# Expert weights of a soft mixture of experts read as 12 KB per partition, with the slots and inner columns reordered

## The chip, the cores and the metric

The kernel runs on one core of one Trainium2 chip. The metric is the device time of one execution in microseconds (us). Three runs of the kernel before gave 594.96, 595.63 and 597.86 us; their median is 595.63 us.

## What is computed

The program computes a causal attention, a soft mixture of experts ("soft MoE") on its output, and a gated two-layer network on that. The change touches the second part only. Cut to what matters:

```python
# N = 1792 tokens, D = 768, E = 8 experts, 4 slots each, F = 1024
logits = x @ phi                          # x: attention output, N x D
d = softmax over tokens of logits
slot_input = (d.T @ x).reshape(E, 4, D)
for e in range(E):
    h = np.maximum(slot_input[e] @ w1[e], 0.0)     # w1[e]: 768 x 1024
    slot_out[e] = h @ w2[e]                        # w2[e]: 1024 x 768
c = softmax over slots of logits
return c @ slot_out                       # goes into the gated network
```

All arrays are float32, except that the three weight matrices of the last network arrive as float64 and are converted on the chip (`from_f64`).

## The kernel before

**Three stages.** Up to about 256 us the attention runs, with an order of steps written out in a table of times (`AT`, `TAIL`, `LOADS`). Its tail ends in `slotT` (lines 630 to 634): six matmuls with `acc` (the sum over tokens, 128 x 768) as stationary operand make the 32 slots' inputs, transposed, 128 rows by six chunks of 32. From there to about 346 us the expert stage runs (lines 754 to 813). After it the gated network runs in six parts (`gate`, `outp`, `prep`).

**Weight pieces.** All weights go through one list, `worder` (lines 156 to 167). Each entry is one DMA of 1536 KB into a tile `w` of 128 x 3072 float32. An expert has four pieces: two of w1 (three chunks of 128 rows each) and two of w2 (four chunks of 128 rows each). I number the pieces in that order: 0 to 3 are expert 0 (w1, w1, w2, w2), and so on to 23, the last of expert 5. Then come 24 to 26, the first w_out, w_val and w_gate of the gated network (unit 0), then 27 to 34 for experts 6 and 7, then unit 1. All are issued by SP (line 181), in this order and pinned to it.

**How a piece lies in memory before.** `w1[e].rearrange("(k p) f -> p k f", p=128)` puts row 128k + p on partition p, so one partition receives three separate rows of 4 KB from each w1 piece, and four rows of 3 KB from each w2 piece.

**Buffers.** The first ten pieces are loaded during the attention, one per step of two head pairs (lines 623 and 624). For the rest `ring` hands out the buffers (lines 170 and 638 to 649): 10 to 14 go into memory that the attention gives back, 15 to 17 into the buffers of 0 to 2, 18 to 24 into those of 3 to 9, 25 to 28 into those of 10 to 13, 29 to 31 into those of 15 to 17, 32 to 34 into those of 18 to 20. So piece 15 waits until the matmuls on piece 0 are done, and piece 17 until those on piece 2 are.

**The matmuls on them.** For each expert (line 757), each of six row chunks kc and each of four column groups g, line 762 multiplies 32 slots with 256 columns of w1 into `psh`: the group g owns partitions 32g to 32g+31. In the trace each of these fp32 matmuls shows as two instructions, and the four groups run side by side; I call four of them that start together a round. Line 765 applies the ReLU and a mask that keeps the expert's own slots; line 768 transposes the result, line 770 copies it out (`hT`), and line 775 multiplies eight chunks of it with the rows of w2, in three column groups, into `so`, which sums over all experts. At the end `so` becomes `soT` (line 813), which the gated network multiplies with its weights (line 688). There the weights are the upper halves of converted float64 values, so the matmul reads every second float32, that is, with a step of 8 bytes.

**The order around it.** The instruction order of each engine comes from a scheduler with a cost model, except for the pinned instructions.

Of the kernel before, what the change touches and what calls it, by code (L numbers as in the profile page):

```python
# [20 lines left out]
def kernel(  # L21
# [13 lines left out]
    nc = tc.nc  # L35
# [6 lines left out]
    KC = DM // 128  # L42
# [71 lines left out]
    g = nc.gpsimd  # L114
# [34 lines left out]
    def w_unit(u):  # L149
        out_ = [(("o", u), w_out.bitcast(I32).rearrange("(k p) f -> p k f", p=128)[:, 2 * u:2 * u + 2, :], 2)]  # L150
        for nm, w in (("v", w_val), ("g", w_gate)):
            src = w.bitcast(I32)[:, 2 * UC * u:2 * UC * (u + 1)]
            out_.append(((nm, u), src.rearrange("(k p) f -> p k f", p=128), KC))
        return out_

    worder = []
    for e in range(E):
        if e == E0:
            for u in PARTS[0]:
                worder += w_unit(u)  # L160
        for r in range(2):
            worder.append((("1", e, r), w1[e].rearrange("(k p) f -> p k f", p=128)[:, 3 * r:3 * r + 3, :], 3))
        for r in range(2):
            worder.append((("2", e, r), w2[e].rearrange("(k p) f -> p k f", p=128)[:, 4 * r:4 * r + 4, :], 4))
    n_ab = len(worder)
    for u in range(len(PARTS[0]), FF // UC):
        worder += w_unit(u)
# [18 lines left out]
    def from_f64(key):  # L186

        t = wt[key].bitcast(I32).rearrange("p a (b w) -> p a b w", w=2)  # L190
        lo, hi = t[:, :, :, 0], t[:, :, :, 1]
        top = wt[key].bitcast(U16).rearrange("p a (b w) -> p a b w", w=4)[:, :, :, 1]

        nc.scalar.activation(out=lo, in_=top, func=AF.Copy, scale=2.0 ** -13, bias=2.0 ** -15 - 0.5)  # L194
        yield
        mult("A", hi.bitcast(F32), hi.bitcast(F32), 2.0 ** -112)
        yield
        nc.vector.scalar_tensor_tensor(lo, hi, -2 ** 31, lo, ALU.bitwise_and, ALU.bitwise_or)  # L198
        yield
        nc.vector.scalar_tensor_tensor(hi, hi, 3, lo, ALU.logical_shift_left, ALU.bitwise_or)  # L200
        yield
        return hi.bitcast(F32)


    with ExitStack() as actx:
# [17 lines left out]
        acc = ac_p.tile([128, DM], F32, name="acc")  # L223
# [28 lines left out]
        fin = {}  # L252
# [377 lines left out]
        slotT = const.tile([128, KC, NS], F32, name="slotT")  # L630
        p4 = psT.tile([128, KC, NS], F32, tag="t", name="psm4")
        for kc in range(KC):
            nc.tensor.matmul(p4[:, kc], lhsT=acc[:, 128 * kc:128 * kc + 128], rhs=fin["fw"], start=True, stop=True)
        nc.vector.tensor_copy(slotT, p4)


# [25 lines left out]
    def prep_o(u, wo):  # L662

        d = unit[u]
        mw = sm1("mw")
        wh = wo_p[u].tile([128, 2, DM], F16, tag=f"wh{(u - 1) % 4}", name="wh")
        wl = wo_p[u].tile([128, 2, DM], F16, tag=f"wl{(u - 1) % 4}", name="wl")
        if MWE[u] == "A":
            nc.scalar.activation(out=wl, in_=wo, func=AF.Abs, accum_out=mw)
        else:  # L670
            nc.vector.tensor_reduce(mw, wo, axis=AX.XY, op=ALU.max, apply_absolute_value=True)
        yield
        am = spread_sum(sm2, ps1, "a", mw)
        d["pw"], sw = pow2(sm2, am, 1, f"w{u}")
        mult(WHE[u], wh, wo, sw)
        yield
        nc.vector.scalar_tensor_tensor(wl, wo, sw, wh, ALU.mult, ALU.subtract)
        d["w"] = (wh, wl)
        yield
# [77 lines left out]
    for e in range(E):  # L757
        ps = ps1.tile([128, 256], F32, tag="a", name="psh")
        for kc in range(KC):
            w = wt["1", e, kc // 3]  # L760
            for g in range(4):
                nc.tensor.matmul(ps[32 * g:32 * g + 32, :], lhsT=slotT[:, kc, :],  # L762
                                 rhs=w[:, kc % 3, 256 * g:256 * g + 256], start=kc == 0, stop=kc == KC - 1)
        hm = hm_p.tile([128, 256], F32, tag="hm", name="hm")
        nc.vector.tensor_scalar(hm, ps, 0.0, emask[:, e:e + 1], ALU.max, ALU.mult)
        pt = ps1.tile([128, 2, 128], F32, tag="b", name="psht")
        for i in range(2):
            nc.tensor.transpose(pt[:, i], hm[:, 128 * i:128 * i + 128], ident)  # L768
        hT = hm_p.tile([128, 2, 128], F32, tag="hT", name="hT")
        nc.scalar.copy(hT, pt)  # L770
        for f in range(8):
            g, i = divmod(f, 2)
            w = wt["2", e, f // 4]
            for c in range(3):
                nc.tensor.matmul(so[32 * c:32 * c + 32, :], lhsT=hT[:, i, 32 * g:32 * g + 32],  # L775
                                 rhs=w[:, f % 4, 256 * c:256 * c + 256],
                                 start=e == 0 and f == 0, stop=e == E - 1 and f == 7)
        if e < B:
            b = e
            cs = cs_p.tile([128, 4, 2, 2, NS], F32, tag="cs", name="cs")  # L780
            chi = hm_p.tile([128, 4, NS], F32R, tag="chi", name="chi")
            c = call[:, b]
            nc.vector.tensor_copy(chi, c)
            ch = chi.bitcast(F32).rearrange("p j (o s) -> p j o s", o=1).to_broadcast([128, 4, 2, NS])
            c4 = c.rearrange("p j (o s) -> p j o s", o=1).to_broadcast([128, 4, 2, NS])
            nc.vector.tensor_copy(cs[:, :, :, 0, :], ch)
            nc.vector.tensor_tensor(cs[:, :, :, 1, :], c4, ch, ALU.subtract)
            ps = ps1.tile([128, S], F32, tag="b", name="psc")
            for j, (s0, n) in enumerate(CH):
                nc.tensor.transpose(ps[:, s0:s0 + n], cs[:n, j].rearrange("p a b s -> p (a b s)"), ident[:n, :n])  # L790
            nc.scalar.copy(cT[:, b * S:(b + 1) * S], ps)
        if e == E0 - 1:
            once.close()
            wo0 = ctx.enter_context(rp("wo0", 1))
            wo_p.update({u: wo0 for u in PARTS[0]})
            w0 = {}
            for u in PARTS[0]:
                for nm in "ovg":
                    f = from_f64((nm, u))
                    while True:  # L800
                        try:
                            next(f)
                        except StopIteration as x:
                            w0[nm, u] = x.value
                            break
                for _ in prep_o(u, w0["o", u]):
                    pass
# [151 lines left out]
```

## Time and profile before

| | |
|---|---|
| median of three runs | 595.63 us |
| shortest, longest | 594.96, 597.86 us |
| span of the profiled execution, first to last instruction | 595.0 us |
| TensorE busy | 514.5 us (86%) |
| VectorE, ScalarE, GpSimd busy | 390.0, 322.6, 238.7 us |
| mean granted TensorE clock | 0.945 of full speed |
| HBM read, written | 95.26 MB, 5.51 MB |
| DMA queue q1 | 95504 packets, 100.77 MB, 51.3% of 16 engines' span |

The profiled execution has no time of its own beside its span; the span is within 0.1 us of the shortest of the three runs and 0.6 us below their median. In the profile PE is TensorE's matmuls, PEld its weight loads, DVE VectorE, ACT ScalarE, POOL GpSimd and SP the engine that issues the DMAs; an engine name with a q at its end (SPq) is that engine's own instruction queue. "L762" is line 762 of the kernel. A DMA share of 1.00 or a little above means that all 16 DMA engines are busy.

### The profile page before, as it was taken

To read this page: it belongs to the slowest core of one execution; us is meant where nothing else is said; L and a number is where in the kernel's file an instruction comes from. 1 tells how busy PE (TensorE), PEld (TensorE's weight loads), DVE (VectorE), ACT (ScalarE), POOL (GpSimd) and SP (SyncE) were. 2 spreads that over 40 slices of the span, in tenths; PEclk is the share of its full clock that TensorE was granted. 3 is DMA by queue.
4 is the path that set the end of the run, shared out by engine and by line. 5 is a ranking of instruction groups with operands and counts; after the bars stand their busy time and mean duration, and the time that the engine had idled before them with its cause. 6 is when DMAs were issued, how large, how long until landed. Compare 5 with 4: busy or idle time off the path is not lost.

```text
span 595.0 us, 12947 instructions
## 1 busy us (share of the span) xinstructions
PE 514.5 (86%) x4971; PEld 317.2 (53%) x4971; DVE 390.0 (66%) x943; ACT 322.6 (54%) x738; POOL 238.7 (40%) x333
## 2 busy tenths in 40 slices
PE   2899989998999899799935689679999989899997
PEld 1576756665667566465512235344554445455654
DVE  3688877886878687331027038986895958675664
ACT  2577767776777577301043049996865843334300
POOL 6654663656365410000000014206696760355720
PEclk9899999999999899979995789998999979799999
DMA  7746557464774313779999993713505303000044
GB/s 161 200 106 170 167 160 199 129 144 133 199 196 115 91 33 107 287 251 391 405 397 405 405 400 137 281 38 119 200 1 209 110 2 107 0 1 1 2 185 186
DMA packets 95566, 101.59 MB, mean 171 GB/s; under 512 B 68625, under 2 KB 68625, under 8 KB 95505
## 3 DMA queue, kind: packets, MB, share of 16 engines
q1 hardware_dynamic: 95504, 100.77, 51.3%
q8 instruction: 39, 0.64, 0.5%
q14 instruction: 23, 0.18, 0.1%
HBM read 95.26 MB, written 5.51 MB: 169 GB/s over the span
## 4 chain that ended last, share of the span: by engine, by line
PE 63%; ACT 15%; DMA 7%; DVE 5%; issue 3%; POOL 2%; SPq 1%; ACTq 0%; DVEq 0%; POOLq 0%
PE pso L870 22%; PE psP L244 9%; PE psS L244 8%; DMA w<-in_moe_w_dram 6%; ACT P L244 4%; PE psX L244 4%; PE psT L244 4%; PE psh L762 3%; PE so L775 3%; ACT hi L244 3%; ACT oacc L144 2%; ACT w L194 2%; PE psg L688 2%; PE psg L843 1%; ACT w L144 1%
## 5 line engine op out<-in xcount | busy, mean ns | idle before, releaser
L852 POOL TENSOR_TENSOR hlo<-hs,hhi 128x448 f16<-128x448 f32 x48 | 59.2, 1241 | 174.9 <-DVE hhi L851 132.5
L870 PE MATMUL pso<-wh,hhi 128*128 128x384 f16 (+1 forms) x384 | 111.5, 338 | 8.1 <-ACT oacc L144 7.6
L870 PE MATMUL pso<-wl,hhi 128*128 128x384 f16 (+1 forms) x384 | 110.3, 334 | 0.0
L870 PE MATMUL pso<-wh,hlo 128*128 128x384 f16 (+1 forms) x384 | 107.8, 331 | 2.6 <-POOL hlo L852 2.6
L244 ACT ACTIVATE P<-psS,nm 128x256 f32<-128x256 f32 (+3 forms) x168 | 82.0, 504 | 31.4 <-PE psP L244 16.6
L870 PEld LDWEIGHTS <-hhi 128*128 128x128 f16 (+1 forms) x768 | 63.5, 103 | 63.8 <-issue 32.3
L244 DVE CUSTOM_DVE_ANT_0 psS<-psS,cmaskq,sc 128x256 f32<-128x256 f32 (+1 forms) x144 | 66.5, 489 | 32.7 <-PE psS L244 30.2
L882 DVE SCALAR_TENSOR_TENSOR oacc<-pso,osc,oacc 128x384 f32<-128x384 f32 x98 | 58.7, 613 | 35.1 <-PE pso L870 34.6
L244 PE MATMUL psP<-ident,P 128*128 128x128 f32 x384 | 59.6, 288 | 17.7 <-ACT P L244 11.6
L880 POOL TENSOR_TENSOR oacc<-oacc,ev 128x384 f32<-128x384 f32 x42 | 55.0, 1321 | 23.1 <-ACT ev L144 23.0
L244 PEld LDWEIGHTS psP<-ident,P 128*128 128x128 f32 x384 | 41.3, 142 | 35.9 <-ACT P L244 21.5
L244 POOL TENSOR_TENSOR sq<-sq 128x512 bf16<-128x512 bf16 (+1 forms) x88 | 56.3, 640 | 6.5
L244 PE MATMUL psV<-PT,v 128*64 128x64 f32 (+3 forms) x672 | 48.0, 293 | 0.3 <-ACT PT L244 0.3
L870 PEld LDWEIGHTS <-hlo 128*128 128x128 f16 (+1 forms) x384 | 34.1, 102 | 26.1 <-issue 3.5
L198 DVE SCALAR_TENSOR_TENSOR w<-w 128x1536 int32<-128x1536 int32 x18 | 33.7, 1874 | 14.5 <-ACT w L144 14.1
L244 PEld LDWEIGHTS psV<-PT,v 128*64 128x64 f32 x672 | 32.0, 137 | 20.9 <-issue 14.0
L144 ACT ACTIVATE ev<-pso,osc 128x384 f32<-128x384 f32 x42 | 23.6, 581 | 27.4 <-PE pso L870 23.7
L194 ACT ACTIVATE w<-w 128x1536 int32<-128x1536 uint16 x18 | 30.2, 1680 | 14.9 <-DMA w<-in_moe_w_out_dram 7.9
L244 POOL TENSOR_SCALAR r<-sum 128x7 f32<-128x7 f32 x24 | 5.9, 244 | 79.1 <-ACT P L244 71.9
L762 PE MATMUL psh<-w,slotT 128*32 128x256 f32 x384 | 29.9, 441 | 7.8 <-DMA w<-in_moe_w_dram 7.3
L244 ACT ACTIVATE hi<-psT,qks 128x448 f16<-128x448 f32 x48 | 27.8, 630 | 15.2 <-PE psT L244 15.2
L770 ACT COPY hT<-psht 128x256 f32<-128x256 f32 x8 | 3.0, 372 | 61.0 <-PE psht L768 61.0
(233 smaller groups left out, 1000.7 us busy)
## 6 DMA issues: line engine op xcount, KB each, us to landing
w<-in_moe_w_dram SPq DMA_DIRECT2D x32, 1536.0 KB, 9.3
w<-in_moe_w_out_dram SPq DMA_DIRECT2D x6, 1536.0 KB, 12.2
w<-in_moe_w_val_dram SPq DMA_DIRECT2D x6, 1536.0 KB, 13.4
w<-in_moe_w_gate_dram SPq DMA_DIRECT2D x6, 1536.0 KB, 6.7
out_dram<-oacc SPq DMA_DIRECT2D x14, 384.0 KB, 2.3
q<-in_q_dram SPq DMA_DIRECT2D x36, 128.0 KB, 3.0
k<-in_k_dram SPq DMA_DIRECT2D x36, 128.0 KB, 2.9
v<-in_v_dram SPq DMA_DIRECT2D x36, 128.0 KB, 8.0
```

What stands on the lines that cost most here:

```text
L144: nc.scalar.activation(out=out, in_=in_, func=AF.Copy, scale=x)
L194: nc.scalar.activation(out=lo, in_=top, func=AF.Copy, scale=2.0 ** -13, bias=2.0 ** -15 - 0.5)
L198: nc.vector.scalar_tensor_tensor(lo, hi, -2 ** 31, lo, ALU.bitwise_and, ALU.bitwise_or)
L244: x = f(*a, **kw)
L688: nc.tensor.matmul(ps[32 * g:32 * g + 32, :], lhsT=soT[:, kc], rhs=w[:, kc], start=kc < 4, stop=kc + 4 >= KC)
L762: nc.tensor.matmul(ps[32 * g:32 * g + 32, :], lhsT=slotT[:, kc, :], rhs=w[:, kc % 3, 256 * g:256 * g + 256], start=kc == 0, stop=kc == KC - 1)
L775: nc.tensor.matmul(so[32 * c:32 * c + 32, :], lhsT=hT[:, i, 32 * g:32 * g + 32], rhs=w[:, f % 4, 256 * c:256 * c + 256], start=e == 0 and ...
L843: nc.tensor.matmul(pg, lhsT=d["g"][:, cols], rhs=cT[:, b * S:(b + 1) * S], start=True, stop=True)
L852: nc.gpsimd.tensor_tensor(lo[:, c], hs, hi[:, c], ALU.subtract)
L870: nc.tensor.matmul(ps[n][o:o + m], lhsT=hid[b, u][x][:, c, s0:s0 + m], rhs=y[:, c, 384 * n:384 * n + 384], start=f, stop=l)
L880: nc.gpsimd.tensor_tensor(a, a, x, ALU.add)
L882: nc.vector.scalar_tensor_tensor(a, ps[n], osc, a, ALU.mult, ALU.add)
```

## The change

```diff
@@ -159,9 +159,9 @@
         for r in range(2):
-            worder.append((("1", e, r), w1[e].rearrange("(k p) f -> p k f", p=128)[:, 3 * r:3 * r + 3, :], 3))
+            worder.append((("1", e, r), w1[e].rearrange("(r p k) f -> r p k f", p=128, k=3)[r], 3))
         for r in range(2):
-            worder.append((("2", e, r), w2[e].rearrange("(k p) f -> p k f", p=128)[:, 4 * r:4 * r + 4, :], 4))
+            worder.append((("2", e, r), w2[e].rearrange("(r p k) f -> r p k f", p=128, k=4)[r], 4))
@@ -630,7 +630,7 @@
         for kc in range(KC):
-            nc.tensor.matmul(p4[:, kc], lhsT=acc[:, 128 * kc:128 * kc + 128], rhs=fin["fw"], start=True, stop=True)
+            nc.tensor.matmul(p4[:, kc], lhsT=acc.rearrange("s (r p k) -> s r k p", p=128, k=3)[:, kc // 3, kc % 3], rhs=fin["fw"], start=True, stop=True)
@@ -759,8 +759,9 @@
             for g in range(4):
-                nc.tensor.matmul(ps[32 * g:32 * g + 32, :], lhsT=slotT[:, kc, :],
-                                 rhs=w[:, kc % 3, 256 * g:256 * g + 256], start=kc == 0, stop=kc == KC - 1)
+                nc.tensor.matmul(ps[32 * g:32 * g + 32, :].rearrange("s (i q) -> s i q", i=2), lhsT=slotT[:, kc, :],
+                                 rhs=w[:, kc % 3].rearrange("p (r q m i) -> p r m i q", m=2, i=2, q=128)[:, g // 2, g % 2],
+                                 start=kc == 0, stop=kc == KC - 1)
```

Row 384r + 3p + k of w1 now lies on partition p, so that a partition receives three neighbouring rows, 12 KB in one stretch; for w2 it is row 512r + 4p + k, four neighbouring rows, again 12 KB. The contraction must meet the same rows on both sides. So the six matmuls of line 633 take every third column of `acc` as stationary operand (a step of 12 bytes), and line 762 takes its moving columns of w1 with a step of four elements (16 bytes), so that `hT` comes out with the inner index that each row of w2 now has. Line 775 is as before. No instruction is added or taken away but the shape of the DMAs; after line 763 the line numbers of the changed kernel are one higher.

On SP the issues of pieces 14 to 18 (buffer numbers in the names, and in brackets what each waits for) stand like this before:

```order
L181 DMA w_4448<-in_moe_w2_dram 128x4x768 [waits DVE_49,PE_49,Activation_49]
L181 DMA w_4450<-in_moe_w2_dram 128x4x768 [waits PE_49]
L181 DMA w_4452<-in_moe_w1_dram 128x3x1024 [waits PE_49]
L181 DMA w_4454<-in_moe_w1_dram 128x3x1024 [waits PE_49]
L181 DMA w_4456<-in_moe_w2_dram 128x4x768 [waits DMAHW3_49]
```

In the changed kernel the same five issues read:

```order
L181 DMA w_4448<-in_moe_w2_dram 128x3072 [waits DVE_49,PE_49,Activation_49]
L181 DMA w_4450<-in_moe_w2_dram 128x3072 [waits PE_49]
L181 DMA w_4452<-in_moe_w1_dram 128x3072 [waits PE_49]
L181 DMA w_4454<-in_moe_w1_dram 128x3072 [waits PE_49]
L181 DMA w_4456<-in_moe_w2_dram 128x3072 [waits DMAHW3_49]
```

Order, buffers and waits are the same; only the shape of the transfer is another, one run of 3072 elements per partition where there were three or four.

On TensorE the start of the expert stage stands like this before, from the matmuls that make `slotT` to the first expert's second half (counts are matmuls, not instructions):

```order
L633 MATMUL psm_4377<-fww,acc 128x32 x6
L762 MATMUL psh<-w,slotT 32x256 x41
L768 MATMUL psht<-ident,hm 128x128 x2
L790 MATMUL psc<-ident,cs 128x128 x3
L790 MATMUL psc<-ident,cs 128x64
L762 MATMUL psh<-w,slotT 32x256 x18
L775 MATMUL so<-w,hT 32x256 x24
```

And in the changed kernel:

```order
L633 MATMUL psm_4377<-fww,acc 128x32 x6
L762 MATMUL psh<-w,slotT 32x256 x41
L769 MATMUL psht<-ident,hm 128x128 x2
L791 MATMUL psc<-ident,cs 128x128 x3
L791 MATMUL psc<-ident,cs 128x64
L762 MATMUL psh<-w,slotT 32x256 x18
L776 MATMUL so<-w,hT 32x256 x24
```

Nothing moved but the line numbers. It is so on all engines, from the first instruction to the last. Before the first matmul on a w2 piece stand 41 + 18 = 59 matmuls on w1 pieces: those of experts 0 and 1, and 11 of expert 2.

## Rows read from the trace of the kernel before

**Rows 1.** The chain that ended last, shares of the span by line.
```profile
PE pso L870 22%; PE psP L244 9%; PE psS L244 8%; DMA w<-in_moe_w_dram 6%; ACT P L244 4%; PE psX L244 4%; PE psT L244 4%; PE psh L762 3%; PE so L775 3%; ACT hi L244 3%; ACT oacc L144 2%; ACT w L194 2%; PE psg L688 2%; PE psg L843 1%; ACT w L144 1%
```

**Rows 2.** The same chain, 255.8 to 346.4: start us, length us, what.
```profile
255.81 2.71 PE psm L633 x12
...
258.95 6.27 PE psh L762 x82
...
266.12 2.07 PE psh L762 x34
...
268.20 0.20 PE psh L762 x2
268.40 3.45 PE so L775 x47
...
297.85 6.29 SPq L181
...
304.23 16.61 DMA w<-in_moe_w_dram
...
320.88 2.63 PE psh L762 x21
323.51 20.76 DMA w<-in_moe_w_dram
...
344.31 1.96 PE so L775 x24
```

**Rows 3.** DMA issues on SP near 261 and 270: start us, us.
```profile
261.81 1.71 SPq L181 DMA_DIRECT2D w<-in_moe_w_dram  x2
...
270.17 1.88 SPq L181 DMA_DIRECT2D w<-in_moe_w_dram  x3
```

**Rows 4.** SP's waits, 268.0 to 271.2: total us, times, longest us.
```profile
SPq L181 <- PE so L775: 6.6, 1, 6.6
```

**Rows 5.** Windows: length, busy us by engine, PEclk, DMA share, GB/s.
```profile
264.60:271.20 6.60, 6.60 (x92) 3.90 (x89) 1.25 (x4) 0.91 (x2) 0.00 (x0) 1.00 1.03 413
271.20:272.40 1.20, 1.20 (x14) 0.64 (x7) 0.00 (x0) 0.14 (x1) 0.00 (x0) 1.00 0.92 222
272.40:300.00 27.60, 26.45 (x381) 15.02 (x379) 3.18 (x8) 2.95 (x7) 0.00 (x0) 1.00 1.03 405
...
320.00:344.30 24.30, 17.33 (x148) 7.01 (x148) 4.02 (x4) 0.74 (x2) 0.00 (x0) 0.65 1.03 405
```

**Rows 6.** DMA in 305.2:309.2 (w_val, w_gate), 293.2:297.2 (w2), 285.7:289.7 (w1), 355.4:357.4 (w_out).
```profile
DMA packets 772, 1.55 MB, mean 387 GB/s; under 512 B 16, under 2 KB 16, under 8 KB 772
...
DMA packets 540, 1.61 MB, mean 402 GB/s; under 512 B 16, under 2 KB 16, under 8 KB 540
...
DMA packets 411, 1.63 MB, mean 408 GB/s; under 512 B 16, under 2 KB 16, under 8 KB 410
...
DMA packets 151, 0.83 MB, mean 417 GB/s; under 512 B 6, under 2 KB 6, under 8 KB 151
```

**Rows 7.** Instructions of lines 762, 688, 633, 790: count, ns min/median/max, first and last start.
```profile
L762 PE MATMUL psh<-w,slotT x384: 379/379/637, 259.0 to 338.3; 128*32 128x256 f32 x192
...
L688 PE MATMUL psg<-w,soT x144: 385/387/418, 347.6 to 530.2; 128*32 128x256 f32 x144
...
L633 PEld LDWEIGHTS psm<-fww,acc x12: 288/333/337, 255.7 to 258.0; 128*128 128x128 f32 x12
...
L790 PEld LDWEIGHTS psc<-ident,cs x16: 134/140/142, 265.3 to 287.5; 128*128 128x128 f32 x12, 64*128 64x128 f32 x4
```

**Rows 8.** TensorE in order of time, two stretches: start us, us, count.
```profile
278.90 1.93 PE L762 MATMUL psh<-w,slotT 128*32 128x256 f32 x32
...
412.91 1.10 PE L688 MATMUL psg<-w,soT 128*32 128x256 f32 x12
```

**Rows 9.** Window of line 762 alone: length, PE and PEld busy, PEclk, DMA.
```profile
258.95:261.70 2.75, 2.75 (x28) 1.38 (x32) 0.50 1.00 399
```

**Rows 10.** The chain after 346.3: shares of that stretch by line.
```profile
by line: PE pso L870 53.7%; ACT oacc L144 5.2%; ACT w L194 4.6%; PE psg L688 4.2%; PE psg L843 3.6%; ACT w L144 3.3%; PE psv L844 3.2%; issue 2.8%; DMA w<-in_moe_w_val_dram 2.6%; ACT wl L669 2.0%; POOL oacc L880 1.8%; DVE w L198 1.7%; DVE h
```

## The prediction

> **What bounds the kernel now.** I read the chain of waits first. Over the whole span it is mostly TensorE; the expert weights' DMA has 6% of it, some 36 us [rows 1]. Read in order of time, that DMA share lies in one place, the second half of the expert stage: from 297.85 to 344.3 us the chain is almost only the issue and the landing of expert pieces, and the stage's last matmuls start when the last w2 piece has landed, at 344.31 [rows 2]. Before that, from 258.95, the chain is TensorE working through experts 0 to 4. The windows say why it changes over: from 272.4 on all 16 DMA engines are busy, at 405 GB/s in both windows shown [rows 5]. So the end of the stage is set by bytes over rate, counted from the last moment at which the DMA engines had nothing to do. That moment is visible: between 271.2 and 272.4 the rate falls to 222 GB/s [rows 5], because piece 17 was issued only at 270.17 [rows 3], after SP had waited 6.6 us for line 775 [rows 4]. This is the release of piece 2's buffer by expert 0's first w2 matmuls. What makes TensorE later before 270 us delays everything behind; what makes the transfers shorter before 270 us is lost in that wait; what makes them shorter after it brings the end of the stage forward. After 346 us the chain is `pso` and ScalarE's work on results and weights [rows 10], which starts from this stage's end, and unit 1's pieces come behind the experts' on the same queue; so a gain or loss is carried to the end of the kernel.
>
> **Part 1, the transfers.** Size and number of the DMAs stay, the run per partition grows from 3 or 4 KB to 12 KB. What that is worth can be read from four stretches in which the engines were all busy with one kind of piece [rows 6]: 387 GB/s with w_val and w_gate (runs of 2 KB), 402 with w2 (3 KB), 408 with w1 (4 KB), 417 with w_out (6 KB). Without the packets under 512 B the counts fit these sizes: 756 packets for 1.55 MB, for instance, is 2 KB each. So with 16 engines one packet takes 16 x 2048 B / 387 GB/s = 84.7 ns, and 122.3, 160.6 and 235.7 ns for the others. From 2 to 6 KB that is 151.0 ns for 4096 B more, 36.9 ns per KB of 1000 B, and about 9 ns that come with each packet. Carried on to 12288 B: 235.7 + 6144 x 0.0369 = 462 ns, or 425 GB/s.
>
> One piece is 1536 KB = 1.573 MB: 3.913 us at 402, 3.855 us at 408, 3.701 us at 425. Behind the gap at 271 us stand pieces 17 to 34. Eight are w2, seven are w1, three belong to unit 0 and don't change. The gain is 8 x 0.212 + 7 x 0.154 = **2.8 us**. No run of 12 KB is in the trace, so the bounds: a packet without any fixed part would give 1000/36.9 x 16 = 434 GB/s, 3.624 us a piece and a gain of 8 x 0.289 + 7 x 0.231 = 3.9 us; the slowest row, 387 GB/s and 4.064 us a piece, would give a loss of 8 x 0.151 + 7 x 0.209 = 2.7 us. I take 2.8, since four rows lie on one line and the nearest of them, 6 KB, is the fastest. Pieces 0 to 9 lie under the attention, 10 to 14 wait for its memory, and 15 and 16 end in the gap: all at nothing.
>
> [...]
>
> **Part 2, the moving reads of w1.** Line 762 now takes its 256 columns with a step of 16 bytes. Contiguous, 32 instructions (eight rounds of four) take 1.93 us [rows 8]; the last shows its own 0.379 us [rows 7], so a round is (1.93 - 0.38) / 7 = 0.221 us. The nearest row with a step is line 688, float32 with 8 bytes: 12 instructions start in four rounds (4, 4, 2, 2) and take 1.10 us [rows 8], the last 0.387 [rows 7], so a round is 0.238 us, 0.017 more. A 16-byte step isn't in the trace. Below I bound it by nothing (no row gives a reason for a gain), above by twice the round, +0.221. I take twice the extra of the 8-byte row, +0.034, since the step doubles. What counts are the rounds ahead of the release at 270 us: 82 + 34 + 2 = 118 instructions [rows 2], of which 28 run at a granted clock of 0.50, in 2.75 us [rows 9], that is 0.39 us a round, where the slower read hardly shows. The other 90 are 22.5 rounds: 22.5 x 0.034 = **0.8 us** later, to 5.0 us at the upper bound, and 0.3 more in the seven slow rounds (7 x (0.442 - 0.39)). Line 762 for later experts is covered: from 297.85 on the chain waits for DMA, and each expert brings four pieces at 3.7 us or more, 14.8 us, against 12 rounds of 0.221 us and 3.45 us of line 775 [rows 2], 6.1 us, or 8.8 with doubled rounds.
>
> **Part 3, the stationary reads of `acc`.** The six matmuls of line 633 take 2.71 us on the chain [rows 2], and their weight loads now step by 12 bytes. Contiguous, their loads show 333 ns, with a granted clock of 0.50 right behind them [rows 9]; those of line 790, of the same size, 140 ns later on [rows 7]. No row has a stationary operand with a step. Bounds: 0 to another 2.7 us. I take the 8-byte row's share, 0.017 / 0.221 = 8% of 2.71, **0.2 us**. It delays the start at 258.95, thus the release too.
>
> **Nothing else.** SP issues the same DMAs with the same waits; line 775 reads w2 in whole rows as before; VectorE, ScalarE and GpSimd keep their instructions.
>
> **Sum.** -2.8 + 0.8 + 0.2 = -1.8 us. The profiled execution has 595.0 us, so 593.2 for one like it; the median of the runs is 0.6 us above, so **593.8 us**. That is -0.3%, less than the 0.5% (3 us) that a measurement of this kernel can tell from no change.
>
> **Rivals.**
>
> 1. *The stepped reads run at half rate (slower).* With each read of four bytes 16 bytes from the last, a round might take 0.442 us. Place: the 118 instructions before 270 us; price 5.3 us, so 595.6 - 2.8 + 5.3 + 0.2 = 598.3 us. If the stationary read is as bad, 2.7 in place of 0.2: 600.8 us. The loss exceeds the gain once a round takes over 0.221 + 2.8/22.5 = 0.345 us. For it: the 8-byte row does cost something, 387 against 379 ns for one instruction and 8% for a round [rows 7, 8]. Against it: 8% is far from double, although that step has already halved what one 16-byte stretch gives. [...]
>
> 2. *Longer runs don't raise the rate.* The 12 KB may be cut into packets of about 4 KB, or another limit may lie just above 408 GB/s. Then only w2 gains, 8 x 0.058 = 0.5 us, against 1.0 of parts 2 and 3: 596.1 us. For it: the step from 4 to 6 KB gave only 9 GB/s. Against it: 417 GB/s was reached.
>
> 3. *All of the gain and no price.* At 434 GB/s and without cost for the reads: 595.6 - 3.9 = 591.7 us. For it: all else is busy elsewhere; against it: line 688.
>
> 4. *12 KB runs are slower than short ones*, at 387 GB/s: 595.6 + 2.7 + 1.0 = 599.3 us. No row points that way.
>
> **Chances.** The forecast 0.45; of it 0.07 falls below 592.65, the bound for faster by over 0.5%. Rival 1 0.20, half of it with the moving reads alone (just inside the 0.5%, with 0.02 beyond), half with both; rival 2 0.17; rival 3 0.14; rival 4 0.04. Faster: 0.14 + 0.07 = 0.21. Slower: 0.10 + 0.02 + 0.04 = 0.16. Within 0.5%: 0.63. The range runs from 591.4, a little below rival 3, to 599.0; it leaves out rival 1 with both reads, most of rival 4 and a little at the lower end.
>
> **What would show it.** In the changed profile the expert stage's DMA windows should show about 425 GB/s with packets over 8 KB; 408 or packets of 4 KB mean rival 2. Line 762 should keep a median near 0.4 us and 32 of its instructions take about 2.2 us; rounds near 0.44 us, an issue of piece 17 some 5 us later and a deeper gap in the DMA there mean rival 1. Line 633 should stay near 2.9 us from first to last. The last w2 matmuls should start some 2 us earlier than 344.3, and what follows should keep its length. I am wrong if line 762 turns up on the chain after 300 us, if the gap at 271 us is not the last one, or if the gain is there at 346 us and gone by the end.

## The result, and the profile after

The changed kernel is slower by 1.2%: a ratio of 1.0122 to the kernel before, 95% interval 1.0082 to 1.0162, some 7 us. Four runs gave 598.94 to 604.16 us, median 601.71; four of before, on the same chip, 592.39 to 597.86, median 595.30. The forecast was 593.8 us with a range up to 599.0. Ratios, here and below, leave out the executions that were slow for their kernel (600.97 to 1210.85 us).

The two profiled executions differ by less, 596.9 against 595.0 us of span. Most of the reason lies ahead of the expert stage: it starts at 255.63 here and at 258.95 before, and one kernel, profiled twice below (runs 3 and 8), started it at 258.77 and at 256.04. So I compare the stage itself, from the first matmul of line 762 to the copy `sos` behind the last w2 matmul: 87.35 us before (258.95 to 346.30), **94.18 us after** (255.63 to 349.81). What follows the copy takes 248.7 us before and 247.0 after. The loss of 6.8 us is in the stage.

The reads of w1 first. The instructions of two lines in the changed kernel (count, ns min/median/max), and a stretch of TensorE in order of time (start us, us, count):

```profile
L762 PE MATMUL psh<-w,slotT x384: 610/632/667, 255.6 to 343.9; 128*32 128x256 f32 x192
...
L633 PEld LDWEIGHTS psm<-fww,acc x12: 252/262/264, 252.7 to 254.6; 128*128 128x128 f32 x12
```

```profile
275.63 3.83 PE L762 MATMUL psh<-w,slotT 128*32 128x256 f32 x32
```

Line 762 went from 379 to 632 ns [rows 7], and a round from 0.221 to (3.83 - 0.63) / 7 = 0.457 us [rows 8]: double. (Taken from the starts of successive rounds it is 0.453 us, against 0.216 before.) Then the DMA, by windows (length, busy us by engine, PEclk, DMA share, GB/s), and the packets from 283 to 290 us:

```profile
263.90:268.20 4.30, 4.30 (x36) 1.55 (x31) 0.63 (x2) 0.90 (x2) 0.00 (x0) 1.00 0.87 369
268.20:273.90 5.70, 5.70 (x66) 3.05 (x60) 0.62 (x2) 0.00 (x0) 0.00 (x0) 1.00 0.01 3
273.90:300.00 26.10, 26.10 (x271) 12.55 (x267) 2.71 (x7) 2.71 (x6) 0.00 (x0) 1.00 1.00 413
```

```profile
DMA packets 274, 2.99 MB, mean 427 GB/s; under 512 B 31, under 2 KB 31, under 8 KB 31
```

The short dip of before [rows 5] has become 5.7 us in which the DMA engines do nothing. After it they run faster than before: 243 packets of 12 KB at 427 GB/s, as forecast. So the last w2 piece lands at 343.9 us by its last packet, against 343.8 before; counted from the stage's start that is 3.4 us later. But the stage doesn't end there. The chain of waits of the changed kernel (start us, us, what):

```profile
255.63 10.13 PE psh L762 x81
...
271.29 3.51 PE so L776 x44
...
291.10 22.23 DMA w<-in_moe_w_gate_dram
313.37 0.06 ACT w L194
...
329.41 1.73 DVE wl L677
331.13 0.41 DVE hm L766
...
332.79 6.04 PE so L776 x45
...
339.04 5.54 PE psh L762 x41
...
346.10 3.69 PE so L776 x48
349.81 0.43 DVE sos L810
```

Where the chain of before goes over two long waits for expert pieces into the last w2 matmuls [rows 2], this one goes through the conversion of unit 0 (lines 194, 144, 198, 200) and the split of its w_out into two float16 parts (line 677), and then over TensorE. The 22.23 us on the DMA of w_gate are only how the profile ascribes the wait that ends at 313.37: w_gate itself is converted from 321.79 on, and the rows below show what ended that wait. The last 48 matmul instructions run in one go, with no wait for the piece that had landed 2.2 us before they begin. ScalarE, VectorE and TensorE in order of time show how it came to that. After:

```profile
313.10 0.37 ACT L771 COPY hT<-psht 128x256 f32<-128x256 f32 x1 [10.35 <-PE psht L769]
313.37 1.66 ACT L194 ACTIVATE w<-w 128x1536 int32<-128x1536 uint16 x1
...
322.30 0.19 PE L139 MATMUL amx<-am,ones 128*128 128x1 bf16 x1 [5.12 <-DVE am L137]
322.42 5.64 PE L762 MATMUL psh<-w,slotT 128*32 128x256 f32 x48
...
329.32 1.81 DVE L677 SCALAR_TENSOR_TENSOR wl<-w,w0s,wh 128x1536 f16<-128x1536 f32 x1
331.05 0.48 DVE L766 TENSOR_SCALAR hm<-psh,emask 128x256 f32<-128x256 f32 x1
```

Before:

```profile
300.07 0.37 ACT L770 COPY hT<-psht 128x256 f32<-128x256 f32 x1 [7.44 <-PE psht L768]
305.11 1.55 ACT L194 ACTIVATE w<-w 128x1536 int32<-128x1536 uint16 x1 [4.67 <-DMA w<-in_moe_w_out_dram]
...
323.74 0.48 DVE L765 TENSOR_SCALAR hm<-psh,emask 128x256 f32<-128x256 f32 x1 [0.69 <-PE psh L762]
```

On ScalarE the first conversion stands behind the copy of expert 5's `hT`. Before, that copy was long done and the conversion waited for its data; now the copy waits 10.35 us for TensorE, and the data of w_out, landed at 305.9, wait for the copy. On TensorE expert 6's matmuls stand behind a one-column matmul of the work on w_out (line 139), for which TensorE waits 5.12 us; before, that one ran at 314.21, ahead of the landing of expert 6's first piece at 317.0, and now that piece, landed at 318.2, waits for it. On VectorE expert 6's ReLU stands behind the last conversion and the split; before it waited for TensorE, now it follows at once, and TensorE stood idle for 3.53 us until it was done.

Something more stands in that stretch. From 331.3 to 338.1 us the granted clock of the changed kernel is 0.50, behind the two idle stretches of 5.12 and 3.53 us:

```profile
331.40:338.00 6.60, 5.90 (x41) 2.67 (x44) 0.13 (x1) 0.37 (x1) 0.00 (x0) 0.50 1.01 426
```

So expert 6's w2 matmuls take 6.04 us for 45 instructions; expert 5's took 3.44 us for as many at 1.00. The kernel before also has 0.50 there, from 309.5 to 330.0 and from 336.8 to 343.6, but its stage ends when the last piece has landed.

The landings of the pieces add the loss up (a piece has landed when its semaphore is complete, some 0.4 us behind its last packet). Piece 17 lands 18.2 us into the stage before and 23.6 after (5.4 later); from there to the landing of piece 34 it takes 67.1 and 65.1 us (2.0 less); from there to the copy `sos` 2.0 and 5.5 us (3.4 more).

### The profile page after: what moved, and what is told of

The parts are those of the page before. It is cut to its first block, busy times and chain, and to the rows that moved or that the text cites. A ratio compares the mean times of both kernels' runs of the same rounds, so it can differ in the third digit from the quotient of the medians.

```text
span 596.9 us, 12947 instructions
## 1 busy us (share of the span) xinstructions
PE 526.5 (88%) x4971; PEld 317.8 (53%) x4971; DVE 388.9 (65%) x943; ACT 322.8 (54%) x738; POOL 238.0 (40%) x333
## 4 chain that ended last, share of the span: by engine, by line
PE 66%; ACT 15%; DVE 7%; issue 4%; DMA 4%; POOL 1%; ACTq 0%; DVEq 0%; POOLq 0%
PE pso L871 25%; PE psP L244 9%; PE psS L244 7%; PE psh L762 5%; ACT P L244 4%; PE psX L244 4%; PE psT L244 4%; DMA w<-in_moe_w_gate_dram 4%; PE so L776 3%; ACT hi L244 3%; ACT w L144 2%; ACT w L194 2%; PE psg L688 2%; ACT oacc L144 1%; PE psv L845 1%
## 5 line engine op out<-in xcount | busy, mean ns | idle before, releaser
L853 POOL TENSOR_TENSOR hlo<-hs,hhi 128x448 f16<-128x448 f32 x48 | 55.3, 1159 | 181.4 <-DVE hhi L852 141.0
L881 POOL TENSOR_TENSOR oacc<-oacc,ev 128x384 f32<-128x384 f32 x42 | 57.5, 1385 | 22.8 <-ACT ev L144 22.7
L244 PEld LDWEIGHTS psP<-ident,P 128*128 128x128 f32 x384 | 41.1, 142 | 35.3 <-ACT P L244 21.0
L762 PE MATMUL psh<-w,slotT 128*32 128x256 f32 x384 | 48.9, 634 | 0.6 <-DVE slotT L634 0.6
L766 DVE TENSOR_SCALAR hm<-psh,emask 128x256 f32<-128x256 f32 x8 | 3.9, 483 | 49.7 <-PE psh L762 49.7
```

The costliest lines, as they stand in the source:

```text
L244: x = f(*a, **kw)
L762: nc.tensor.matmul(ps[32 * g:32 * g + 32, :].rearrange("s (i q) -> s i q", i=2), lhsT=slotT[:, kc, :], rhs=w[:, kc % 3].rearrange("p (r q ...
L853: nc.gpsimd.tensor_tensor(lo[:, c], hs, hi[:, c], ALU.subtract)
L881: nc.gpsimd.tensor_tensor(a, a, x, ALU.add)
```

## The experiments

Each stage length below is from one profile; the two profiles of one kernel, runs 3 and 8, differ by 0.3 us.

Theory A: the change loses by the 16-byte step of the moving reads alone, and the longer transfers gain what was forecast. Theory B: the longer transfers themselves do harm. T is the kernel before on the same chip.

**1. Only w1 in runs of 12 KB.**

```diff
 # against the change
-w2[e].rearrange("(r p k) f -> r p k f", p=128, k=4)[r]
+w2[e].rearrange("(k p) f -> p k f", p=128)[:, 4 * r:4 * r + 4, :]
...
-rhs=w[:, kc % 3].rearrange("p (r q m i) -> p r m i q", m=2, i=2, q=128)[:, g // 2, g % 2]
+rhs=w[:, kc % 3, 256 * g:256 * g + 256]
```

> Only w1 is read with 12 KB per partition; line 762 reads contiguous columns again, w2 stays at 3 KB. Theory A (the 16-byte step of line 762 costs the time, the transfers gain): rounds of line 762 back at 0.22 us, seven w1 pieces behind the gap shorter by 0.15 us each, time T - 1 us (T is the kernel before on this chip). Theory B (the longer transfers themselves cost the time): about half the loss remains, T + 3.5 us.

Ratio 1.0003 (0.9982 to 1.0025); the stage takes 87.0 us. The loss is gone with the step, as A says. Of the gain only 0.4 of 1.1 us shows (more on that at run 7). This kernel keeps the stationary reads of `acc` with 12 bytes:

```profile
L633 PEld LDWEIGHTS psm<-fww,acc x12: 288/329/330, 255.7 to 258.0; 128*128 128x128 f32 x12
```

That is 329 ns against 333 contiguous [rows 7], so the step of a stationary operand costs nothing here, where the granted clock is 0.50. At 1.00 it does cost. In the changed kernel these loads ran at 1.00 and show the 262 ns above; in run 7, with `acc` contiguous, they ran at 1.00 too:

```profile
L633 PEld LDWEIGHTS psm<-fww,acc x12: 186/192/242, 253.2 to 254.5; 128*128 128x128 f32 x12
```

With the step the loads start 174 ns apart, without it 111; at 0.50 it is 213 ns either way. From first to last the six matmuls take 2.28 us in the changed kernel and 1.66 in run 7. This lies ahead of the stage as I measure it.

**2. Only the step, with the old transfers.**

```diff
 # against the kernel before
-rhs=w[:, kc % 3, 256 * g:256 * g + 256]
+rhs=w[:, kc % 3].rearrange("p (r q m i) -> p r m i q", m=2, i=2, q=128)[:, g // 2, g % 2]
```

> The kernel before, with transfers of 4 and 3 KB, but line 762 reads with the step of 16 bytes; which hidden column meets which row of w2 is therefore permuted, and the output is another. Theory A: the whole loss and none of the gain, T + 8 to T + 10 us, rounds of 0.46 us, the DMA gap near 271 us some 5 us longer. Theory B: T, within 1 us.

Ratio 1.0121 (1.0081 to 1.0161), stage 94.3 us, line 762 with a median of 632 ns. The step alone makes the whole loss; B falls. But I expected 8 to 10 us and 7 came: with the step, the stage is as long with transfers of 12 KB as with 3 and 4 KB, though the last piece lands 88.7 us into it with the former and 91.7 with the latter. The faster DMA is worth nothing once TensorE and the conversions set the end.

**3 and 8. The change with pairs.** Line 762 reads two neighbours, then goes on 16 bytes; the two transposes per expert sort the columns.

```diff
 # against the change
-nc.tensor.matmul(ps[32 * g:32 * g + 32, :].rearrange("s (i q) -> s i q", i=2), lhsT=slotT[:, kc, :],
-                 rhs=w[:, kc % 3].rearrange("p (r q m i) -> p r m i q", m=2, i=2, q=128)[:, g // 2, g % 2],
+nc.tensor.matmul(ps[32 * g:32 * g + 32, :].rearrange("s (q i) -> s q i", i=2), lhsT=slotT[:, kc, :],
+                 rhs=w[:, kc % 3].rearrange("p (r q m i) -> p r m q i", m=2, i=2, q=128)[:, g // 2, g % 2],
-nc.tensor.transpose(pt[:, i], hm[:, 128 * i:128 * i + 128], ident)
+nc.tensor.transpose(pt[:, i], hm.rearrange("s (q i) -> s i q", i=2)[:, i], ident)
```

> The change, but line 762 reads its columns in the order (q, i) instead of (i, q): two neighbouring floats, then 16 bytes further, and the step moves to the two transposes per expert (8 bytes). Theory A in the form that what counts is a new 16-byte stretch for each element: rounds as in line 688, 0.24 us, packets of 12 KB at 425 GB/s, time T - 2.5 us. Theory A in the form that any step of 16 bytes costs: rounds above 0.35 us, T + 2 us or more. Theory B: T + 6 us.

> The same kernel as the third run, for a closer interval: T - 2 us, a ratio of 0.9965, if what the profile shows (stage shorter by 2.4 us) is all of it; 1.000 if the 2.4 us are lost behind the stage.

The first time 0.9970 (0.9937 to 1.0004), which just reaches no change, the second 0.9959 (0.9928 to 0.9989): **faster than both kernels**, than the one before by some 2 us. The stage takes 85.0 and 85.3 us. In the second profile, line 762, a window of the DMA, and the last w2 matmuls:

```profile
L762 PE MATMUL psh<-w,slotT x384: 385/389/637, 256.0 to 334.1; 128*32 128x256 f32 x192
```

```profile
275.00:300.00 25.00, 23.37 (x328) 13.94 (x323) 2.08 (x5) 2.56 (x6) 0.00 (x0) 1.00 1.01 421
```

```profile
339.34 1.93 PE L776 MATMUL so<-w,hT 128*32 128x256 f32 x24 [1.07 <-DMA w<-in_moe_w_dram]
```

The matmul is at 389 ns, near line 688's 387 [rows 7]; the end of the stage waits for the DMA again, and the DMA has the higher rate (421 GB/s, against 405 before [rows 5]).

**4. A step for each expert.**

```diff
 # against the kernel before, line 762
+st = (1, 4, 2, 3, 8, 0, 1, 1)[e]
+fl = w.rearrange("p a b -> p (a b)")
+o = min(1024 * (kc % 3), 3072 - 256 * max(st, 1)) if st != 1 else 1024 * (kc % 3) + 256 * g
-rhs=w[:, kc % 3, 256 * g:256 * g + 256]
+rhs = fl[:, o:o + 256 * st:st] if st else fl[:, 1024 * (kc % 3):1024 * (kc % 3) + 512].rearrange("p (q m i) -> p m q i", m=2, i=2)[:, g % 2]
...
```

> The kernel before; line 762 reads its 256 columns with another step for each expert, so the products are other ones: 4 bytes for experts 0, 6 and 7, 16 for 1, 8 for 2, 12 for 3, 32 for 4, pairs (two neighbours, then 16 bytes on) for 5. If a new 16-byte stretch costs about 1.8 ns each and hides under the 213 ns of the columns: rounds of 0.22, 0.46, 0.24, about 0.35, 0.46 and 0.24 us in that order. If the distance counts: 32 bytes about twice 16 bytes, 0.9 us, and pairs like 12 bytes. No forecast of the time.

The matmul in six windows, in the order 16, 8, 12, 32 bytes, pairs, 4 bytes (count, ns min/median/max):

```profile
L767 PE MATMUL psh<-w,slotT x30: 629/632/663, 261.4 to 265.1; 128*32 128x256 f32 x30
...
L767 PE MATMUL psh<-w,slotT x20: 386/390/415, 274.2 to 275.2; 128*32 128x256 f32 x20
...
L767 PE MATMUL psh<-w,slotT x32: 507/512/539, 280.8 to 283.2; 128*32 128x256 f32 x32
...
L767 PE MATMUL psh<-w,slotT x38: 629/639/643, 287.6 to 291.8; 128*32 128x256 f32 x38
...
L767 PE MATMUL psh<-w,slotT x43: 385/388/404, 302.2 to 304.5; 128*32 128x256 f32 x43
...
L767 PE MATMUL psh<-w,slotT x20: 379/379/403, 338.0 to 338.9; 128*32 128x256 f32 x20
```

In the trace the starts of successive rounds lie 453, 226, 340, 460, 226 and 216 ns apart. The 256 columns touch 256, 128, 192, 256, 128 and 64 stretches of 16 bytes. 453/256, 340/192 and 226/128 are all 1.77 ns; 64 x 1.77 = 113 ns would lie below the columns' own 216. It is the number of 16-byte stretches that costs, neither the step (32 bytes cost hardly more than 16) nor its being a step (pairs cost what 8 bytes cost). They count in the order of the reads: the change's 256 columns lie in 128 stretches, but it goes over them twice, one column of each at a time, and its round takes 0.453 us like that of 256. The price doesn't follow the granted clock either: at 0.50, from 256.2 to 259.6 us, the changed kernel's rounds start 0.45 us apart too, where contiguous ones start 0.43 apart at 0.50 and 0.216 at 1.00. The weight loads of run 1 fit as well: 128 columns at 12 bytes touch 96 stretches, and 96 x 1.77 = 170 ns is near the 174 at a clock of 1.00 and below the 213 at 0.50.

**5 and 6. The step in one half of the experts.** The other half reads contiguous columns; the output is another.

```diff
 # against the change; run 5 with e < 2, run 6 with e >= 2
+rhs = w[:, kc % 3].rearrange("p (r q m i) -> p r m i q", m=2, i=2, q=128)[:, g // 2, g % 2]
+if not (e < 2):
+    rhs = w[:, kc % 3, 256 * g:256 * g + 256].rearrange("p (i q) -> p i q", i=2)
...
```

> The change, but only experts 0 and 1 read w1 with the 16-byte step; the others read contiguous columns, so their hidden columns meet other rows of w2 and the output is another. If the loss is all in the late release of the buffers (theory A1): T + 7 us. If it is all in TensorE being late for experts 5 to 7 (A2): T - 2 us. My reading of the changed trace, both halves: the release of piece 2 some 5 us later, so a DMA gap of some 5 us, then the DMA is the bound again to the end of the stage, less 2.8 us: T + 2 to T + 3 us.

> The other half: experts 2 to 7 read w1 with the 16-byte step, experts 0 and 1 contiguously (another output, as before). A1: T - 2.5 us. A2: T + 7 us. My reading: piece 17 as early as in the kernel before, the last w2 piece lands 2 to 3 us earlier, but TensorE is some 10 us late at expert 5, the conversions of the gated network's first weights start that much later, and expert 6's ReLU stands behind them on VectorE: T to T + 2 us, with the last w2 piece landed several us before it is used.

Early: 1.0036 (1.0005 to 1.0067), stage 89.6 us, 2.3 above before. Late: 1.0014 (0.9985 to 1.0042), stage 88.7 us, 1.3 above. Both times come as I read them; A1 and A2 fall as sole causes. The window of the gap, first in the early kernel, then in the late one:

```profile
268.30:274.40 6.10, 6.10 (x81) 3.47 (x73) 0.62 (x2) 0.17 (x1) 0.00 (x0) 1.00 0.23 53
```

```profile
268.30:274.40 6.10, 6.10 (x68) 3.21 (x65) 0.63 (x2) 0.91 (x2) 0.00 (x0) 1.00 0.67 234
```

The early kernel has the gap; at its end the stage waits for the DMA. In the late one piece 17 starts 2.7 us earlier than in the early one (270.4 against 273.1 by its first packet) and the last piece has landed at 340.4, but the ReLU of expert 6 follows the conversions at once, and the last matmuls start only at 340.97, after that landing. My reading of this run missed in two places: counted from the stage's start, piece 17 is issued 2.2 us later than before and not as early, of which 1.3 us are the step in 11 of the 59 matmuls ahead of it (5.5 rounds at 0.236), and the last piece lands only 0.5 us earlier.

```profile
325.46 1.81 DVE L677 SCALAR_TENSOR_TENSOR wl<-w,w0s,wh 128x1536 f16<-128x1536 f32 x1
327.19 0.48 DVE L768 TENSOR_SCALAR hm<-psh,emask 128x256 f32<-128x256 f32 x1
```

Each half also holds the transfers' gain. If it is the forecast's 2.8 us, the prices are 2.3 + 2.8 = 5.1 and 1.3 + 2.8 = 4.1 us; both less one gain make 6.4, near the 6.8 of the change; with the 2.1 to 2.4 us of runs 3 and 8 they make 5.7 to 6.0.

**7. Only w2 in runs of 12 KB, with pairs.** As run 3, with w1 and `acc` as before.

```diff
 # against run 3
-w1[e].rearrange("(r p k) f -> r p k f", p=128, k=3)[r]
+w1[e].rearrange("(k p) f -> p k f", p=128)[:, 3 * r:3 * r + 3, :]
```

> Only w2 is read with 12 KB per partition, w1 in rows of 4 KB as before, and line 762 reads pairs as in the third run. Eight w2 pieces behind the gap, 0.21 us each, less 0.3 us for the rounds: T - 1.5 us. If the order of long and short packets matters more than their mean (only w1 long gave 0.4 us of the 1.1 forecast): T - 0.5 us.

Ratio 0.9977 (0.9952 to 1.0001), stage 86.4 us, 0.9 shorter: between the two forecasts, and the interval just reaches 1. With run 1 the halves give 0.4 and 0.9 us of stage, together less than the 2.1 to 2.4 of both. But this isn't shown to be a loss by mixing, since in the profile of before the same transfers are quicker than in other runs. From the landing of piece 17 to that of piece 34 it takes 67.1 us; runs 2, 4 and 10, with the same transfers, take 67.7, 67.8 and 67.8. Run 1 takes 67.0, run 7 66.1, and the six traces with both, the changed kernel and runs 3, 5, 6, 8 and 9, take 64.7 to 65.2. Against the mean of the four old ones, 67.6, the gains are 0.6, 1.6 and 2.4 to 2.9 us, where the forecast's 0.154 and 0.212 us a piece make 0.9, 1.7 and 2.6 for these 17 pieces.

**9 and 10. Without the conversions.**

```diff
 # against the change (9) and against the kernel before (10)
-f = from_f64((nm, u))
...
-w0[nm, u] = x.value
+w0[nm, u] = wt[nm, u].bitcast(I32).rearrange("p a (b w) -> p a b w", w=2)[:, :, :, 1].bitcast(F32)
```

> The change without the six ScalarE and six VectorE operations that convert the first w_out, w_val and w_gate (the raw upper words are used instead, so the output is another); everything else, the order of the rest included, is as in the change. If the conversions, which start only behind expert 5's copy and stand in front of expert 6's matmuls and ReLU, are what keeps the end of the stage behind the last w2 piece: the stage ends 2 us after that piece lands, some 4 us earlier than in the change, T + 3 us. If TensorE's own doubled rounds set the end: within 1 us of the change, T + 7 us.

> The control: the kernel before without the same twelve operations. There the last experts wait for their weights, and the conversions fit into that wait: the stage keeps its length, T within 1 us. If the conversions delay the stage in any case: T - 4 us.

The stage of the change falls from 94.2 to 91.1 us, and its last matmuls wait for the DMA again. That row, and the window in which the changed kernel had a clock of 0.50:

```profile
345.42 1.93 PE L776 MATMUL so<-w,hT 128*32 128x256 f32 x24 [1.00 <-DMA w<-in_moe_w_dram]
...
331.40:338.00 6.60, 4.08 (x42) 1.17 (x36) 0.00 (x0) 0.00 (x0) 0.00 (x0) 1.00 1.01 423
```

Two runs of it give 596.45 and 596.75 us against a median of 593.92, T + 2.7, too few for an interval; so the reading rests on the stage. The control gave 0.9995 (0.9962 to 1.0027), stage 87.9 us. So the conversions cost the change 3.1 us of its stage and the kernel before nothing. What they cost directly, by standing in front of expert 6's matmuls and ReLU, and what the half clock behind that wait adds, these runs don't separate: without the conversions the clock stays at 1.00.

## Why the prediction was wrong

- **What bounds the kernel**: right for the kernel before, with the gap at 271 us as the place where TensorE's lateness passes to the DMA. That this bound would stay was taken for granted, and it didn't. The sign named for being wrong, line 762 on the chain after 300 us, could not tell: the chain of before has it already, 2.63 us at 320.88 [rows 2].
- **Part 1, transfers**: right. 462 ns a packet and 425 GB/s were forecast; the trace has 427 GB/s, with 16 engines 460 ns a packet. A piece was to take 3.70 us; in a stretch of 12 KB runs alone (pieces 27 to 29 of the changed kernel) the landings are 3.69 and 3.70 us apart. Runs 3 and 8 earn it: 2.1 to 2.4 us in the stage with the pairs' small price in it.
- **Part 2, moving reads: the step that failed.** "I take twice the extra of the 8-byte row, +0.034, since the step doubles": measured, a round takes 0.457 us, +0.236. The 8-byte row was read as a small surcharge, where it is a limit that has just come through: 128 stretches at 1.77 ns are 226 ns, a little over the columns' 216. Double the stretches, and it is the limit that doubles (453 ns for 256 in run 4). The upper bound, twice the round, was the right value, and rival 1 with its place and its doubled round was the case that came (it priced the lateness at the release at 5.3 us, and piece 17 lands 5.4 us later); its 0.20 was too little. What was held against it, that the 8-byte row costs only 8% (5% by the starts, 226 against 216 ns), says nothing of a step of 16 bytes: that row reads two float32 of each 16-byte stretch, and run 4 shows 226 ns a round with two and 453 with one.
- **"Line 762 for later experts is covered"** failed too, and it makes rival 1's price too small: 598.3 us, where the ratio puts the change some 7 us over before. The cover was counted as four pieces' time against one expert's matmuls. It left out that on ScalarE and VectorE unit 0's conversions stand between expert 5's copy and expert 6's ReLU. TensorE at expert 5 is 16 us later (copy of `hT` 57.5 against 41.1 us into the stage), so the wait in which the conversions were free is used up. Run 9 prices that, with the half clock that comes with it, at 3.1 us.
- **Part 3, stationary reads**: forecast 0.2 us as 8% of 2.71, at a granted clock of 0.50; measured nothing at that clock (run 1). At 1.00, as in the changed kernel's profile, the step costs 0.6 us over the six matmuls (2.28 against 1.66 us in run 7).
- **The base**: 595.0 us was taken as a time, but runs take some 2 us more than their span (598.94 for 596.9). That did not move the forecast, which is the median of the runs less 1.8 us.

## What to carry to other kernels

When a layout makes DMA runs longer, look at what it does to the innermost step of every matmul operand that streams: count the 16-byte stretches that its elements touch, in the order of the reads (the float32 reads of run 4 cost 1.77 ns for each, against 216 ns for their 256 columns), and keep two float32 of each together where only one order in a stretch needs to change. A row with a milder form of a cost gives no slope to carry on: ask which limit it has just crossed. And work that is "covered by the DMA" is covered only as long as what stands behind it on the other engines has slack; check the order of work on each engine, not only the totals.

## What the runs showed of the hardware

In run 4 the moving float32 reads of line 762's matmul (line 767 there) go at 1.77 ns per 16-byte stretch in each of four column groups, once that is more than the 216 ns of their 256 columns (granted clock 1.00): 226 ns for 128 stretches, 340 for 192, 453 for 256, and 460 with 32 bytes between elements. At 0.50 a round of 256 stretches takes 0.45 us too (the changed kernel, 256.2 to 259.6 us), a contiguous one 0.43 (the kernel before). Weight loads with a step of 12 bytes start 174 ns apart at 1.00 (the changed kernel), contiguous ones 111 (run 7); at 0.50 both start 213 ns apart (run 1 and the kernel before). Packets of 12 KB move at 427 GB/s in the changed kernel, within 0.5% of what the straight line through the packet times of 2, 3, 4 and 6 KB gives (425 GB/s, from 387, 402, 408 and 417).
